# Retention feeding a four-expert attention layer: the queries and keys of two experts in the two halves of the rows

## The chip, the cores and the metric

The kernel runs on one core of a Trainium2 chip. Its metric is the device time of one launch in microseconds (us), by the median of several runs. A profile of one execution gives the engines' instructions: PE is TensorE's matmuls, PEld its loads of stationary tiles, DVE VectorE, ACT ScalarE, POOL GpSimd, and SP the engine that issues the DMAs.

## What is computed

A retention layer (a decaying running state per head) gives x. A mixture of four attention experts, of which two count for each token, gives the output. B = 4 batches, H = 8 heads, S = 768 tokens, D = 64; the model width is 512, and an expert's head width Hd is 64.

```python
def _attn_ref(q, k, v):
    gamma = 1.0 - 2.0 ** (-5.0 - np.arange(H, dtype=np.float32))
    for t in range(S):
        state = gamma[None, :, None, None] * state + np.einsum('bhd,bhe->bhde', k[:, :, t], v[:, :, t])
        y[:, :, t] = scale * np.einsum('bhd,bhde->bhe', q[:, :, t], state)
...
def _moe_ref(x, w_gate, wq, wk, wv, wo):
    logits = x @ w_gate
    ...
    for e in range(E):
        q = x @ wq[e]
        k = x @ wk[e]
        v = x @ wv[e]
        scores = scale * (q @ k.transpose(0, 2, 1))
        scores = np.where(causal, -1000000000.0, scores)
        scores = scores - scores.max(-1, keepdims=True)
        a = np.exp(scores)
        a /= a.sum(-1, keepdims=True) + 1e-09
        ye = a @ v @ wo[e]
        ...
            out += mask[..., None] * w[:, :, kk:kk + 1] * ye
```

## The kernel before

The tokens are worked in eight stages j of HS = 384 (NJ = 8; an odd stage is the second half of its batch), each of three chunks of 128. The experts go in two pairs p.

Precision comes from splitting: a factor is held as a rounded part (hi, type fp32r) and the rest (lo), and products are summed as hi*hi + hi*lo + lo*hi. Plain fp32 matmuls stay in the retention and in the attention's last product; a plain fp32 matmul is issued as two instructions.

The steps, with their lines:

- `h1`, `h2`, `kturn` (L405 to L549): the retention, in 64x64 tiles, four of them to the array.
- `proj` (L599): queries and keys of one expert together, 128 output rows, 12 matmuls of 384 columns. ACT rounds q (L605) and k (L607) out of the bank, DVE takes the rests (L610, L613), and copies on POOL and ACT (L625, L627) bring q and k into the other half of the rows, so that one 128-row matmul gives (k_hi + k_lo) times q_hi.
- `vgate` (L650): values and gate logits, 260 columns.
- `mpass` (L731, L744, L745): the score rows again with tokens of q on the partitions, one expert at a time, for each row's maximum, which DVE takes out of the bank (L734, L753). `mrow` (L781 to L787) turns the maxima into a row through DRAM; in the last stage matmuls (L774) do it.
- `score` (L857, L858): for each block of 128 keys and each expert, two matmuls; the second, of 65 rows, adds k_hi times q_lo and subtracts the maximum through a row of ones. ACT takes the exponential (L864): 384-wide blocks once per expert, narrower ones for both experts in one bank and one instruction.
- `av` (L905), `norm_a`, `norm_b`, `wout` (L1031): the product with v, the sums, the normalisation, the output.

`Recorder.op` collects these steps with their dependencies, and `schedule` emits them in the order of the table `ORDER`, found offline and written out by number. All engines' streams, the DMA queue of SP included, follow that one order; tiles of a pool go to whoever comes next in it. Seven PSUM banks (`ps`) serve all but the retention's state. Every PE step carries a `mode`: the shape into which the array is divided, such as 128x128 or 64x64 (rows x columns of one tile).

Of the kernel before, what the change touches and what calls it, by code (L numbers as in the profile page):

```python
# [252 lines left out]
def tile_retention_moe_attention(  # L253
# [330 lines left out]
    def proj(j, p, e):  # L584
# [724 lines left out]
```

## Time and profile before

| | us |
|---|---|
| median of 3 runs (lowest, highest) | 328.93 (328.56, 329.5) |
| profiled execution | 330.6 |
| its span | 328.7 |
| PE, PEld busy | 315.1, 279.2 |
| DVE, POOL, ACT busy | 200.7, 180.4, 162.2 |

The span is the part of the profiled execution between its first and its last instruction; 1.9 us lie around it. Shares of busy time are means over the whole span. A matmul's row shows its time through the array, so rows of following matmuls overlap; how long one holds the next up is the distance between their starts.

### The profile page before, as it was taken

The numbers are of one execution on the slowest core, as the hardware profiler recorded it, in microseconds if no ns is written. First come the engines' busy times: TensorE is split into PE (matmuls) and PEld (weight loads), VectorE is DVE, ScalarE is ACT, GpSimd is POOL, SyncE is SP. The second block draws the span as 40 slices with busy tenths as digits, with TensorE's granted clock in tenths as the row PEclk, the third lists the DMA queues.
The fourth block names the chain that finished last, engine by engine and source line by source line (L and its number), as shares of the span: only waits on it lengthen the run. The fifth ranks groups of instructions, "written<-read, shape, count | busy, mean of one in ns | idle before, by whom it ended". The sixth has DMA issues, their size and how long they took to land.

```text
span 328.7 us, 11866 instructions
## 1 busy us (share of the span) xinstructions
PE 315.1 (96%) x5060; PEld 279.2 (85%) x5060; DVE 200.7 (61%) x538; ACT 162.2 (49%) x376; POOL 180.4 (55%) x206
## 2 busy tenths in 40 slices
PE   4797999999999999999999999999999999999995
PEld 4487999998997899998997899988998899877673
DVE  2772588788744454595657255677564276688653
ACT  1410455463566255554553625564674417857532
POOL 2674344544398691946278964681397912816300
PEclk9997999999999999999999999999999999999999
DMA  6978272150723522553406322144300112013012
GB/s 222 353 251 256 68 255 69 71 181 23 237 75 131 163 74 95 210 122 95 130 10 223 133 76 81 54 162 152 84 1 4 50 38 71 15 61 79 35 64 96
DMA packets 15880, 37.54 MB, mean 114 GB/s; under 512 B 2034, under 2 KB 6214, under 8 KB 15828
## 3 DMA queue, kind: packets, MB, share of 16 engines
q1 hardware_dynamic: 15828, 36.79, 34.1%
q8 instruction: 39, 0.64, 0.7%
q14 instruction: 13, 0.11, 0.1%
HBM read 29.99 MB, written 6.79 MB: 112 GB/s over the span
## 4 chain that ended last, share of the span: by engine, by line
PE 92%; DMA 4%; DVE 1%; issue 1%; SPq 0%; ACT 0%; ACTq 0%
PE ps L599 21%; PE ps L905 11%; PE ps L650 11%; PE ps L1031 11%; PE ps L857 7%; PE ps L858 6%; PE ps_st L484 5%; PE ps L549 5%; DMA kv_t<-in_kv_dram 4%; PE ps L745 4%; PE ps L731 2%; PE ps L488 2%; PE ps L543 2%; PE ps L941 2%; PE ps L744 1%
## 5 line engine op out<-in xcount | busy, mean ns | idle before, releaser
L864 ACT ACTIVATE pt<-ps 128x384 f32<-128x384 f32 (+2 forms) x112 | 50.0, 491 | 19.2 <-PE ps L858 15.4
L753 DVE CUSTOM_DVE_ANT_0 scr<-ps,cmask 128x256 bf16<-128x256 f32 (+3 forms) x64 | 30.2, 486 | 35.9 <-PE ps L745 35.7
L599 PE MATMUL ps<-xh,qk_hi 128*128 128x384 f32 x128 | 44.6, 348 | 0.0
L599 PE MATMUL ps<-xl,qk_hi 128*128 128x384 f32 x128 | 43.5, 340 | 0.0
L599 PE MATMUL ps<-xh,qk_lo 128*128 128x384 f32 x128 | 43.5, 340 | 0.0
L857 PE MATMUL ps<-q,k 128*128 128x384 f32 (+2 forms) x144 | 43.5, 318 | 0.0
L858 PE MATMUL ps<-q,k 65*128 65x384 f32 (+2 forms) x144 | 42.5, 312 | 0.0
L905 PE MATMUL ps<-pt,vt 64*64 64x384 f32 (+2 forms) x576 | 41.7, 415 | 0.0
L886 POOL TENSOR_TENSOR ac<-ac,pt 128x256 f32<-128x256 f32 (+2 forms) x32 | 40.0, 1252 | 1.6
L438 POOL TENSOR_TENSOR qd<-qkT_t,tabs 128x512 f32<-128x512 f32 (+1 forms) x23 | 28.6, 1243 | 22.1 <-PE ps L488 18.1
L870 POOL TENSOR_SCALAR_AFFINE_SELECT pt<-pt 128x256 f32<-128x256 f32 x48 | 19.6, 418 | 27.3 <-ACT pt L864 23.2
L549 PE MATMUL ps<-qkT_t 64*64 64x64 f32 x768 | 28.1, 223 | 5.2 <-DMA qkT_t<-in_qkT_dram 4.9
L905 PEld LDWEIGHTS ps<-pt,vt 64*64 64x64 f32 x576 | 21.9, 133 | 12.1 <-issue 8.7
L549 PEld LDWEIGHTS ps<-qkT_t 64*64 64x64 f32 x768 | 26.0, 138 | 5.8 <-DMA qkT_t<-in_qkT_dram 4.9
L484 PE MATMUL ps_st<-kv_t 64*64 64x64 f32 x704 | 29.4, 221 | 0.6 <-DVE kv_t L423 0.3
L498 DVE TENSOR_TENSOR sblk<-ps_st,tabs 128x256 f32<-128x256 f32 x44 | 18.5, 421 | 18.6 <-PE ps_st L484 17.7
L484 PEld LDWEIGHTS ps_st<-kv_t 64*64 64x64 f32 x704 | 24.9, 134 | 5.7 <-issue 3.6
L650 PE MATMUL ps<-vg_hi,xl 128*128 128x260 f32 x96 | 27.6, 288 | 1.9 <-issue 1.9
L605 ACT ACTIVATE q<-ps 64x384 fp32r<-64x384 f32 x32 | 15.4, 480 | 28.0 <-PE ps L599 27.9
L488 PE MATMUL ps<-qd,sblk 64*64 64x64 f32 x704 | 29.2, 221 | 0.0
L857 PEld LDWEIGHTS ps<-q,k 128*128 128x128 f32 x144 | 27.4, 190 | 1.9 <-issue 0.9
L511 ACT ACTIVATE xh<-ps 128x512 fp32r<-128x512 f32 x24 | 14.3, 597 | 28.4 <-PE ps L488 28.2
(129 smaller groups left out, 838.0 us busy)
## 6 DMA issues: line engine op xcount, KB each, us to landing
qkT_t<-in_qkT_dram SPq DMA_DIRECT2D x24, 512.0 KB
kv_t<-in_kv_dram SPq DMA_DIRECT2D x23, 512.0 KB
out_dram<-ot SPq DMA_DIRECT2D x21, 256.0 KB
fe<-fd SPq DMA_DIRECT2D x28, 96.0 KB
pt<-in_wqk_dram SPq DMA_DIRECT2D x4, 256.0 KB
out_dram<-ot SPq DMA_DIRECT2D x6, 128.0 KB
...
```

What stands on the lines that cost most here:

```text
L484: nc.tensor.matmul(ST[b].t[rows(rt), s * D:(s + 1) * D], kvs(m, 0, s)[rows(rt)], kvs(m, 1, s)[rows(rt)], start=c == 0 and s == 0, stop=Fal ...
L488: nc.tensor.matmul(yo(m, rt, s), SB[m % 2][rows(rt), s], LD[g, 2].t[rows(rt), s, m % 2 * SC:(m % 2 + 1) * SC], start=m % 2 == 0 and s == 0 ...
L549: nc.tensor.matmul(ps.t[rows(rt), a:a + SC], qb.t[rows(rt), 1, s, t], qb.t[rows(rt), 0, s, t], start=True, stop=True)
L599: nc.tensor.matmul(pb.t[:, :HS], ww[:, kt, wsl], xx[:, kt], start=n == 0, stop=n == 11)
L650: nc.tensor.matmul(pb.t[:, :NV + E], xx[:, kt, sl], ww[:, kt], start=n == 0, stop=n == 11)
L753: lambda: nc.vector.tensor_tensor_reduce(scr.t[:, :n1], pb.t[:, :n1], K["cmask"][:, HS + C - n1:], 1.0, mx0.t[:, e, i:i + 1] if prior else ...
L857: nc.tensor.matmul(o, k1.t[:, e, ko:ko + C], q1.t[:, e, q0:], start=True, stop=False)
L858: nc.tensor.matmul(o, k2.t[:65, e, ko:ko + C], q2.t[:65, e, q0:], start=False, stop=True)
L864: lambda es=es, sb=sb, n=n: nc.scalar.activation(pt.t[:, es[0]:es[0] + n, q0:], sb.t[:, :n * w].rearrange("p (e t) -> p e t", e=n), AF.Exp ...
L886: op(eng, cost, lambda: en.tensor_tensor(ac.t[:, :, q0:], ac.t[:, :, q0:], pt.t[:, :, q0:], op=OP.add), r=[(pt, 0), (pt, 1), (ac, "b")], w ...
L905: nc.tensor.matmul(ob.t[e * 64:e * 64 + 64, q0:HS], VTB[kj].t[rr, ko // C, ee * 64:ee * 64 + 64], PTB[j, p, kb].t[rr, e, q0:], start=kb == ...
L1031: nc.tensor.matmul(wb.t, oo[:, sl], ww[:, p], start=n == 0 and p == 0, stop=n == 2 and p == NP - 1)
```

## The change

Queries of both experts of a pair are projected together, one expert into the upper 64 rows and the other into the lower; keys likewise (`_layouts` orders the weights so). Each projection is rounded by one ACT instruction over 128 rows and its rest is taken by one on DVE; the copies to the other half go. The pools Q1, Q2, K1, K2 of two experts' width become QH, QL, KH, KL of one. `mpass` and `score` issue matmuls of 64 rows in pairs, expert 0 from the upper rows into one bank and expert 1 from the lower rows into another; their shape is 64x128. `mpass` uses q_hi times k_hi alone. `score` has four steps: hi*hi, lo of q, lo of k, and a tile with one row of ones for each expert (`oner`) times the negated maxima (`mr`, two buffers, filled by two DMAs in place of one). The exponential is always one instruction per expert. In the last stage one set of three matmuls and one ACT copy brings both experts' maxima. The tiles for the exponentials (`pt`) grow from 8 to 12. `SUB` is empty, so its branches are never taken. The table of the order is new throughout.

```diff
-    Q1 = tag("q1", 3, [128, 2, HS], F32R)
...
+    QH = tag("qh", NQ, [128, HS], F32R)
+    QL = tag("ql", NQ, [128, HS], F32R)
+    KH = tag("kh", NK, [128, HS], F32R)
+    KL = tag("kl", NK, [128, HS], F32R)
+    MR = tag("mr", 2, [128, HS], F32R)
...
-    def proj(j, p, e):
+    def proj(j, p, t):
...
-        op("ACT", act_c(HS), lambda: nc.scalar.activation(q1.t[up, e], pb.t[up, :HS], AF.Copy), r=[(pb,)],
-           w=[(q1, "a", e)])
-        op("ACT", act_c(HS), lambda: nc.scalar.activation(k1.t[low, e], pb.t[low, :HS], AF.Copy), r=[(pb,)],
-           w=[(k1, "h", e)])
...
+        op("ACT", act_c(HS), lambda: nc.scalar.activation(th.t, pb.t[:, :HS], AF.Copy), r=[(pb,)], w=[(th,)])
+        op("DVE", dve_c(HS), lambda: nc.vector.tensor_tensor(tl.t, pb.t[:, :HS], th.t, op=OP.subtract),
+           r=[(pb,), (th,)], w=[(tl,)])
...
-    def mpass(j, p, e, i):
+    def mpass(j, p, i):
...
+        def mm(o, k, e, n):
+            nc.tensor.matmul(o, qh.t[rows(e), i * C:(i + 1) * C], k.t[rows(e), :n], start=True, stop=True)
...
+            for e in range(2):
+                mm(pb[e].t[:, n0:n1], kb, e, n)
+
+        op("PE", max(n * COL, 0.11) + n0 * COL + 0.01, fn, r=[(qh,), (kb,)] + ([(ka,)] if both else []),
+           w=[*[(x,) for x in pb], (mx, "n")], new=pb + ([mx] if new else []), mode="64x128", ni=8 if both else 4)
...
     def score(j, p, kb):
...
-                    nc.tensor.matmul(o, k1.t[:, e, ko:ko + C], q1.t[:, e, q0:], start=True, stop=False)
-                    nc.tensor.matmul(o, k2.t[:65, e, ko:ko + C], q2.t[:65, e, q0:], start=False, stop=True)
...
+            steps = [(kk[x].t, qq[y].t, ko) for x, y in ((0, 0), (0, 1), (1, 0))] + ([] if sub else [(oner, m.t, 0)])
+            for n, (k, q, o) in enumerate(steps):
+                for e in range(2):
+                    nc.tensor.matmul(sb[e].t[:, :w], k[rows(e), o:o + C], q[rows(e), q0:], start=n == 0,
+                                     stop=n == len(steps) - 1)
...
-        for es in ([(0, 1)] if w <= 256 else [(0,), (1,)]):
-            sb = Buf(PB)
-            n = len(es)
...
+            for e in range(2):
+                op("ACT", act_c(w),
+                   lambda e=e: nc.scalar.activation(pt.t[:, e, q0:], sb[e].t[:, :w], AF.Exp, scale=isc),
+                   r=[(sb[e],)], w=[(pt, e)])
...
     def mrow(j, p):
...
-            for e in range(2):
-                pb = Buf(PB)
...
-                    for i in range(CH):
-                        nc.tensor.matmul(pb.t[:65, i * C:(i + 1) * C], mz.t[:, e, i], nid, start=True, stop=True)
...
+                for i in range(CH):
+                    nc.tensor.matmul(pb.t[:65, i * C:(i + 1) * C], mz.t[:, i], nid, start=True, stop=True)
...
+            for e in range(2):
+                op("SP", 0.4,
+                   lambda e=e: nc.sync.dma_start(
+                       o.t[64 * e:64 * e + 1].bitcast(F32),
+                       md.t[e * CH:(e + 1) * CH].rearrange("c t -> (c t)")[None, :]),
+                   r=[(md,), ("mr0",)], w=[(o, e)], new=[] if e else [o], nbytes=1536)
...
 ORDER = """
-1 5 2 4 108 9 3 6 13 17 11 7 8 14 19 88 12 24 0 26 25 18 28 10 42 27 15 29 66 31 34 16 30 71 43 44 38 75 32 39 45 40
...
+6 1 22 2 5 3 4 9 13 12 19 14 7 17 8 11 88 18 24 87 0 26 25 20 10 42 27 36 15 28 75 29 43 66 31 38 16 32 30 40 39 37 44
...
```

What the new table does is seen in the built programs' streams. TensorE, maxima next to projections: before, two matmuls of `mpass` (L745, one expert each) stand between two projections (L599), all of 128x128.

```order
L599 MATMUL ps_141<-xh_73,qk_hi 128x384
L599 MATMUL ps_141<-xl_75,qk_hi 128x384
L599 MATMUL ps_141<-xh_73,qk_lo 128x384
L745 MATMUL ps_143<-k_0_82,q_0_76 128x384
L745 MATMUL ps_145<-k_0_82,q_0_76 128x384
L599 MATMUL ps_140<-xh_73,qk_hi 128x384
L599 MATMUL ps_140<-xl_75,qk_hi 128x384
L599 MATMUL ps_140<-xh_73,qk_lo 128x384
```

After, between two projections (L588) of a later stage (the last three and the first two rows of them), `mpass` (L685) issues two pairs; with qh and kh one row follows the other into two banks. One pair is over the stage's own keys (kh_87), the other over the half before (kh_85).

```order
L588 MATMUL ps_153<-xh_73,qk_hi 128x384
L588 MATMUL ps_153<-xl_75,qk_hi 128x384
L588 MATMUL ps_153<-xh_73,qk_lo 128x384
L685 MATMUL ps_152<-kh_87,qh_78 128x384
L685 MATMUL ps_151<-kh_87,qh_78 128x384
L685 MATMUL ps_150<-kh_85,qh_78 128x384
L685 MATMUL ps_149<-kh_85,qh_78 128x384
L588 MATMUL ps_148<-xh_72,qk_hi 128x384
L588 MATMUL ps_148<-xl_74,qk_hi 128x384
```

The maxima have moved out of a run of one shape into an island of their own: 128x128, 64x128, 128x128.

TensorE, scores: before, a stretch of `score` of the second stage, one bank for both experts at 256 columns, one for each at 384, then two maxima of a later stage; all of 128x128.

```order
L857 MATMUL ps_139<-q_1_77,k_1_83 128x256
L858 MATMUL ps_139<-q_1_80,k_1_88 128x256
L857 MATMUL ps_139<-q_1_77,k_1_83 128x256
L858 MATMUL ps_139<-q_1_80,k_1_88 128x256
L857 MATMUL ps_142<-q_1_77,k_1_83 128x384
L858 MATMUL ps_142<-q_1_80,k_1_88 128x384
L857 MATMUL ps_144<-q_1_77,k_1_83 128x384
L858 MATMUL ps_144<-q_1_80,k_1_88 128x384
L745 MATMUL ps_145<-k_2_84,q_2_78 128x384
L745 MATMUL ps_140<-k_2_84,q_2_78 128x384
```

After, one block of `score` (L832, 128 keys by 384 queries) with maxima (L685) ahead and behind: four steps, each once per expert, and all of 64x128.

```order
L685 MATMUL ps_148<-kh_85,qh_78 128x384
L685 MATMUL ps_149<-kh_85,qh_78 128x384
L832 MATMUL ps_151<-qh_79,kh_84 128x384
L832 MATMUL ps_152<-qh_79,kh_84 128x384
L832 MATMUL ps_151<-ql_83,kh_84 128x384
L832 MATMUL ps_152<-ql_83,kh_84 128x384
L832 MATMUL ps_151<-qh_79,kl_89 128x384
L832 MATMUL ps_152<-qh_79,kl_89 128x384
L832 MATMUL ps_151<-mr_94,oner 128x384
L832 MATMUL ps_152<-mr_94,oner 128x384
L685 MATMUL ps_147<-kh_87,qh_78 128x256
L685 MATMUL ps_150<-kh_87,qh_78 128x256
```

Two matmuls per expert and block have become four of half the rows, and maxima stand beside scores in the same shape.

SP, the first DMAs: before, the tables (L333) and two chunks of q and k (L382) lead, then half of the first k and v (L386) and the weights (L351).

```order
L333 DMA tabs<-in_tabs_dram 128x368
L382 DMA qkT_t_63<-in_qkT_dram 128x1024
L382 DMA qkT_t_64<-in_qkT_dram 128x1024
L386 DMA kv_t_66<-in_kv_dram 128x512
L351 DMA ac_117<-in_wvg_dram 128x260
L351 DMA pt_109<-in_wqk_dram 128x512
```

After, that half of the first k and v (L380) leads.

```order
L380 DMA kv_t_66<-in_kv_dram 128x512
L326 DMA tabs<-in_tabs_dram 128x368
L376 DMA qkT_t_63<-in_qkT_dram 128x1024
L376 DMA qkT_t_64<-in_qkT_dram 128x1024
L344 DMA ac_125<-in_wvg_dram 128x260
L344 DMA ot_135<-in_wvg_dram 128x260
```

It has moved ahead of the tables (L326) and of the first q and k (L376).

## Rows read from the trace of the kernel before

**Rows 1.** The page, engines (busy us, share, instructions), and the chain by engine.

```profile
PE 315.1 (96%) x5060; PEld 279.2 (85%) x5060; DVE 200.7 (61%) x538; ACT 162.2 (49%) x376; POOL 180.4 (55%) x206
...
PE 92%; DMA 4%; DVE 1%; issue 1%; SPq 0%; ACT 0%; ACTq 0%
```

**Rows 2.** Stretches: length, busy us (instructions) by engine, clock, DMA share, GB/s.

```profile
0.00:40.00 40.00, 30.43 (x691) 26.67 (x695) 18.97 (x37) 10.35 (x22) 20.48 (x30) 0.96 0.71 236
40.00:285.00 245.00, 245.00 (x4042) 223.61 (x4035) 152.59 (x418) 128.84 (x299) 147.82 (x161) 1.00 0.31 103
```

**Rows 3.** Waits of TensorE: sum in us, times, longest.

```profile
PE ps L549 <- DMA qkT_t<-in_qkT_dram: 4.9, 1, 4.9
PE ps L650 <- issue: 1.9, 1, 1.9
PE ps L1179 <- DVE xl L514: 1.8, 1, 1.8
```

**Rows 4.** Timeline of TensorE (start us, length): from 64x64 into 128x128.

```profile
59.48 0.22 PE L488 MATMUL ps<-qd,sblk 64*64 64x64 f32 x1
59.62 0.44 PE L857 MATMUL ps<-q,k 128*128 128x384 f32 x1
59.90 0.34 PE L858 MATMUL ps<-q,k 65*128 65x384 f32 x1
60.08 0.34 PE L731 MATMUL ps<-k,q 128*128 128x384 f32 x1
```

**Rows 5.** The same view: 256 columns, then from 128x128 into 64x64.

```profile
58.67 0.28 PE L857 MATMUL ps<-q,k 128*128 128x256 f32 x1
58.78 0.28 PE L858 MATMUL ps<-q,k 65*128 65x256 f32 x1
59.00 0.27 PE L484 MATMUL ps_st<-kv_t 64*64 64x64 f32 x1
```

**Rows 6.** The same view: 128 columns in a row.

```profile
101.80 0.28 PE L858 MATMUL ps<-q,k 65*128 65x128 f32 x1
101.91 0.28 PE L857 MATMUL ps<-q,k 128*128 128x128 f32 x1
```

**Rows 7.** Matmuls of the maxima: line, shape, count, busy us, mean ns.

```profile
L731 PE MATMUL ps<-k,q 128*128 128x384 f32 x32 | 10.8, 359 | 0.0
L745 PE MATMUL ps<-k,q 128*128 128x128 f32 (+2 forms) x96 | 24.3, 295 | 0.0
L744 PE MATMUL ps<-k,q 128*128 128x384 f32 x16 | 5.6, 367 | 0.0
```

**Rows 8.** Timeline of TensorE: groups of four 64x64 matmuls.

```profile
59.10 0.22 PE L484 MATMUL ps_st<-kv_t 64*64 64x64 f32 x1
59.11 0.22 PE L488 MATMUL ps<-qd,sblk 64*64 64x64 f32 x1
59.12 0.22 PE L484 MATMUL ps_st<-kv_t 64*64 64x64 f32 x1
...
59.16 0.22 PE L484 MATMUL ps_st<-kv_t 64*64 64x64 f32 x1
```

**Rows 9.** Timeline of the weight loads (PEld): the same groups.

```profile
59.16 0.14 PEld L484 LDWEIGHTS ps_st<-kv_t 64*64 64x64 f32 x1
...
59.22 0.14 PEld L484 LDWEIGHTS ps_st<-kv_t 64*64 64x64 f32 x1
```

**Rows 10.** Groups of ACT and DVE: exponential, evacuation of a projection.

```profile
L864 ACT ACTIVATE pt<-ps 128x384 f32<-128x384 f32 x80 | 35.5, 492 | 11.9 <-PE ps L858 10.4 <-DVE mx L753 0.5 <-POOL pt L870 0.3
L613 DVE TENSOR_TENSOR k<-ps,k 64x384 fp32r<-64x384 f32 x32 | 17.7, 559 | 6.5 <-ACT k L607 4.4 <-ACT q L605 1.4
L605 ACT ACTIVATE q<-ps 64x384 fp32r<-64x384 f32 x32 | 15.4, 480 | 28.0 <-PE ps L599 27.9
```

**Rows 11.** Stretches around the stop of TensorE at 26.5 us.

```profile
26.50:28.60 2.10, 0.22 (x3) 0.01 (x2) 0.00 (x0) 0.00 (x0) 0.11 (x1) 1.00 0.90 267
28.60:32.00 3.40, 3.40 (x12) 3.40 (x13) 0.00 (x0) 0.00 (x0) 1.94 (x2) 0.50 0.98 272
```

More of the change, by code (lines that the diff above doesn't have):

```diff
@@ L28 @@
 WARM = 8
-PACE = ()
-QP = True
-KP = False
+SUB = ()
+NQ = 4
 IDLE = (2, 4)
@@ L373, in tile_retention_moe_attention @@
     nid = sbuf.tile([128, 128], F32R, name="nid")
+    oner = sbuf.tile([128, 128], F32R, name="oner")
     K = {}
@@ L582, in stream_r @@
         return u
[L584 removed]
+    def proj(j, p, t):
         xh, xl = XT[j]
         hi, lo = W["qk"]
[L588 to L593 removed]
+        wsl = slice((p * 2 + t) * 128, (p * 2 + t + 1) * 128)
+        pb = Buf(PB)
+        th, tl = (KT if t else QT)[j, p] = (Buf(KH), Buf(KL)) if t else (Buf(QH), Buf(QL))
         def fn():
@@ L600, in fn @@
                     n += 1
-        op("PE", 12 * HS * COL, fn, r=xtok(xh) + xtok(xl) + wtok("qk"),
-           w=[(pb,), *[(t, "n") for t in (q1, q2, k1, k2)]], new=[pb, *new], mode="128x128", ni=24)
-        up, low = slice(0, 64), slice(64, 128)
-        op("ACT", act_c(HS), lambda: nc.scalar.activation(q1.t[up, e], pb.t[up, :HS], AF.Copy), r=[(pb,)],
-           w=[(q1, "a", e)])
-        op("ACT", act_c(HS), lambda: nc.scalar.activation(k1.t[low, e], pb.t[low, :HS], AF.Copy), r=[(pb,)],
-           w=[(k1, "h", e)])
-        op("DVE", dve_c(HS),
-           lambda: nc.vector.tensor_tensor(q2.t[up, e], pb.t[up, :HS], q1.t[up, e], op=OP.subtract),
-           r=[(pb,), (q1, "a", e)], w=[(q2, "x", e)])
-        op("DVE", dve_c(HS),
-           lambda: nc.vector.tensor_tensor(k1.t[up, e], pb.t[low, :HS], k1.t[low, e], op=OP.subtract),
-           r=[(pb,), (k1, "h", e)], w=[(k1, "q", e)])
-        each = j == NJ - 1
-        if not e and not each:
-            return
-        es = [e] if each else range(2)
-        a, b = es[0], es[-1] + 1
-        n = len(es) * HS
-        def turn(pool, d, s, r, w):
-            if pool:
-                op("POOL", pool_c(n), lambda: nc.gpsimd.tensor_copy(d(), s()), r=r, w=w)
-            else:
-                op("ACT", act_c(n), lambda: nc.scalar.activation(d(), s(), AF.Copy), r=r, w=w)
-        turn(QP and not each, lambda: q1.t[low, a:b], lambda: q1.t[up, a:b], [(q1, "a", y) for y in es],
-             [(q1, "b", y) for y in es])
-        turn(KP and not each, lambda: k2.t[up, a:b], lambda: k1.t[low, a:b], [(k1, "h", y) for y in es] + [("k2ones",)],
-             [(k2, "x", y) for y in es])
-    def qtok(j, p, e):
-        return [(QT[j, p][0], "a", e), (QT[j, p][0], "b", e)]
-    def ktok(j, p, e):
-        return [(KT[j, p][0], "q", e), (KT[j, p][0], "h", e)]
+        op("PE", 12 * HS * COL, fn, r=xtok(xh) + xtok(xl) + wtok("qk"), w=[(pb,), (th, "n"), (tl, "n")],
+           new=[pb, th, tl], mode="128x128", ni=24)
+        op("ACT", act_c(HS), lambda: nc.scalar.activation(th.t, pb.t[:, :HS], AF.Copy), r=[(pb,)], w=[(th,)])
+        op("DVE", dve_c(HS), lambda: nc.vector.tensor_tensor(tl.t, pb.t[:, :HS], th.t, op=OP.subtract),
+           r=[(pb,), (th,)], w=[(tl,)])
     def vgate(j, i):
@@ L722, in mpass @@
         mx, mx0 = MXB[j, p]
-        q1 = QT[j, p][0]
-        def lhs():
-            return q1.t[:, e, i * C:(i + 1) * C]
-        if half and i:
-            pa = Buf(PB)
-            ka = KT[j - 1, p][0]
-            op("PE", HS * COL, lambda: nc.tensor.matmul(pa.t[:, :HS], lhs(), ka.t[:, e], start=True, stop=True),
-               r=qtok(j, p, e) + ktok(j - 1, p, e), w=[(pa,), (mx0, "n")], new=[pa, mx0] if (e, i) == (0, 1) else [pa], mode="128x128", ni=2)
-            op("DVE", dve_c(HS),
-               lambda: nc.vector.tensor_reduce(mx0.t[:, e, i:i + 1], pa.t[:, :HS], axis=AX.X, op=OP.max),
-               r=[(pa,)], w=[(mx0, e, i)])
+        qh, kb = QT[j, p][0], KT[j, p][0]
@@ new lines, in mpass, with fa @@
+        ka = KT[j - 1, p][0] if half else None
+        def mm(o, k, e, n):
+            nc.tensor.matmul(o, qh.t[rows(e), i * C:(i + 1) * C], k.t[rows(e), :n], start=True, stop=True)
+        prior = half and i
+        if prior:
+            pa = [Buf(PB) for _ in range(2)]
+            def fa():
+                for e in range(2):
+                    mm(pa[e].t[:, :HS], ka, e, HS)
+            op("PE", HS * COL + 0.01, fa, r=[(qh,), (ka,)], w=[*[(x,) for x in pa], (mx0, "n")],
+               new=[*pa, mx0] if i == 1 else pa, mode="64x128", ni=4)
+            for e in range(2):
+                op("DVE", dve_c(HS),
+                   lambda e=e: nc.vector.tensor_reduce(mx0.t[:, e, i:i + 1], pa[e].t[:, :HS], axis=AX.X, op=OP.max),
+                   r=[(pa[e],)], w=[(mx0, e, i)])
@@ L736, in mpass @@
         n = (i + 1) * C
-        pb, scr = Buf(PB), Buf(SCR)
-        kb = KT[j, p][0]
         both = half and not i
         n0 = HS if both else 0
+        n1 = n0 + n
+        pb = [Buf(PB) for _ in range(2)]
         def fn():
             if both:
-                nc.tensor.matmul(pb.t[:, :HS], lhs(), KT[j - 1, p][0].t[:, e], start=True, stop=True)
-            nc.tensor.matmul(pb.t[:, n0:n0 + n], lhs(), kb.t[:, e, :n], start=True, stop=True)
-        n1 = n0 + n
-        op("PE", max(n * COL, 0.11) + n0 * COL, fn,
-           r=qtok(j, p, e) + ktok(j, p, e) + (ktok(j - 1, p, e) if both else []), w=[(pb,), (mx, "n"), (scr, "n")],
-           new=[pb, scr] + ([mx] if new else []), mode="128x128", ni=4 if both else 2)
@@ L751, in mpass @@
-        prior = half and i
-        op("DVE", dve_c(n1) + 0.05,
-           lambda: nc.vector.tensor_tensor_reduce(scr.t[:, :n1], pb.t[:, :n1], K["cmask"][:, HS + C - n1:], 1.0,
-                                                  mx0.t[:, e, i:i + 1] if prior else NEG, op0=OP.add, op1=OP.max,
-                                                  accum_out=mx.t[:, e * CH + i:e * CH + i + 1]),
-           r=[(pb,), ("cmask_t",)] + ([(mx0, e, i)] if prior else []), w=[(mx, e, i), (scr,)])
+                for e in range(2):
+                    mm(pb[e].t[:, :HS], ka, e, HS)
@@ new lines, in fn @@
+            for e in range(2):
+                mm(pb[e].t[:, n0:n1], kb, e, n)
+        op("PE", max(n * COL, 0.11) + n0 * COL + 0.01, fn, r=[(qh,), (kb,)] + ([(ka,)] if both else []),
+           w=[*[(x,) for x in pb], (mx, "n")], new=pb + ([mx] if new else []), mode="64x128", ni=8 if both else 4)
+        for e in range(2):
+            scr = Buf(SCR)
+            op("DVE", dve_c(n1) + 0.05,
+               lambda e=e, scr=scr: nc.vector.tensor_tensor_reduce(
+                   scr.t[:, :n1], pb[e].t[:, :n1], K["cmask"][:, HS + C - n1:], 1.0,
+                   mx0.t[:, e, i:i + 1] if prior else NEG, op0=OP.add, op1=OP.max,
+                   accum_out=mx.t[:, e * CH + i:e * CH + i + 1]),
+               r=[(pb[e],), ("cmask_t",)] + ([(mx0, e, i)] if prior else []), w=[(mx, e, i), (scr,)], new=[scr])
@@ L799, in stream_p @@
             for i in range(CH):
-                for e in range(2):
-                    mp[p].append((COST["m1"] if half else COST["m0"], lambda p=p, e=e, i=i: mpass(j, p, e, i)))
+                mp[p].append((COST["m1"] if half else COST["m0"], lambda p=p, i=i: mpass(j, p, i)))
             mp[p].append((COST["mrow"], lambda p=p: mrow(j, p)))
@@ new lines, in score, with fn @@
+        sub = j in SUB
+        sb = [Buf(PB) for _ in range(2)]
+        def fn():
+            steps = [(kk[x].t, qq[y].t, ko) for x, y in ((0, 0), (0, 1), (1, 0))] + ([] if sub else [(oner, m.t, 0)])
+            for n, (k, q, o) in enumerate(steps):
+                for e in range(2):
+                    nc.tensor.matmul(sb[e].t[:, :w], k[rows(e), o:o + C], q[rows(e), q0:], start=n == 0,
+                                     stop=n == len(steps) - 1)
+        op("PE", (3 if sub else 4) * max(w * COL, 0.11) + 0.01, fn,
+           r=[(x,) for x in (*kk, *qq)] + ([] if sub else [(m, 0), (m, 1) if j < NJ - 1 else (m, 0), ("oner",)]),
+           w=[*[(x,) for x in sb], (pt, "n")], new=[*sb, pt], mode="64x128", ni=4 * (3 if sub else 4))
@@ new lines, in score @@
+        if sub:
+            for e in range(2):
+                op("DVE", dve_c(w),
+                   lambda e=e: nc.vector.tensor_tensor(pt.t[:, e, q0:], sb[e].t[:, :w], m.t[:, e, q0:], op=OP.add),
+                   r=[(sb[e],), (m, e)], w=[(pt, e)])
+            op("ACT", act_c(2 * w),
+               lambda: nc.scalar.activation(pt.t[:, :, q0:], pt.t[:, :, q0:], AF.Exp, scale=isc),
+               r=[(pt, 0), (pt, 1)], w=[(pt, 0), (pt, 1)])
+        else:
+            for e in range(2):
+                op("ACT", act_c(w),
+                   lambda e=e: nc.scalar.activation(pt.t[:, e, q0:], sb[e].t[:, :w], AF.Exp, scale=isc),
+                   r=[(sb[e],)], w=[(pt, e)])
@@ L1216, in head, with mkone, mkmr @@
         wsplit(2)
-        for t in K2.tiles:
-            op("POOL", 0.73, lambda t=t: nc.gpsimd.memset(t[64:65].bitcast(F32), 1.0), w=[("k2ones",)])
+        def mkone():
+            nc.gpsimd.memset(oner.bitcast(F32), 0.0)
+            for e in range(2):
+                nc.gpsimd.memset(oner[64 * e:64 * e + 1].bitcast(F32), 1.0)
+        def mkmr():
+            for t in MR.tiles:
+                nc.gpsimd.memset(t.bitcast(F32), 0.0)
+        op("POOL", 0.6, mkone, w=[("oner",)])
+        op("POOL", 1.5, mkmr, w=[("mr0",)])
     head()
```

79 lines of the change are left out of this document (32 added, 47 removed), and 110 rows, old and new, of the table ORDER.

## The prediction

> **What bounds the kernel now.** I read the shares of the engines and the chain first, then the stretches, then the waits, and last the distances from one matmul's start to the next. TensorE is busy 96% of the span and carries 92% of the chain; the next engine, VectorE, has 61% [rows 1]. The stretches sharpen this: from 40 to 285 us TensorE is busy 245.00 of 245.00 us at a granted clock of 1.00, the 2.4 GHz level, while 40.00 less 30.43 = 9.6 us of its idle time lie in the first 40 us [rows 2], half of it the wait for the first load [rows 3]. So no wait is worth removing in the middle: only columns that TensorE no longer streams, or columns and pauses that it gains, move the end there. A busy row hides pauses, since a matmul's row outlasts the start of the next, so every price below is a distance between starts.
>
> **Prices of a matmul.** With 384 columns the next one starts 0.18 us later [rows 4]; with 256 columns 0.12 [rows 5]; with 128 columns 0.11 and not 0.06 [rows 6]. So a step costs its columns, or 0.11 us if that is more, which is the load of a 128-wide stationary tile.
>
> **Maxima (mpass): shorter.** Before, one expert at a time: 80 matmuls of 384 columns (L731 32, L744 16, a third of L745's 96), 32 of 256 and 32 of 128 (the other thirds) [rows 7]. 80 x 0.176 + 32 x 0.118 + 32 x 0.11 = 14.1 + 3.8 + 3.5 = 21.4 us, all on the path. After, the two experts sit in the two halves of the rows and write two banks. If both run at once, 10.7 us go. Are they at once? The 64x64 matmuls of the retention start four to a group, 0.01 us apart, and the next group follows 0.06 us after the first [rows 8], so the halves of the rows do work side by side there. Their loads do too: four fit into 0.06 us [rows 9], and a first load alone shows as 0.04 to 0.05 where nothing hides it (below). No row shows it for fp32r with 128 columns, hence rivals below.
>
> **Scores: even.** Before, each expert had two matmuls per key block (k_hi + k_lo times q_hi; k_hi times q_lo with the maximum as a 65th row). After, both experts have four (hi*hi, hi*lo, lo*hi, ones times maximum), each on 64 rows, two at a time: four steps per key block either way, 40 blocks of 384 columns, 16 of 256, 16 of 128. Twice as many matmuls are issued, but 0.01 us apart as above; I take 0.
>
> **The last stage's maxima:** 12 matmuls of 128 columns become 6: 6 x 0.11 = 0.7 us less.
>
> **Changes of shape: longer.** TensorE stops between shapes. Coming into 128x128 at 59.62, the first start is 0.14 us behind the last of a group that would have followed after 0.04, and the second comes 0.28 us on where later steps take 0.18 [rows 4]: 0.10 + 0.10 or 0.11, about 0.21 in all. Coming into 64x64 at 59.00, 0.22 instead of 0.12, and then 0.10 instead of 0.06 [rows 5, 8]: 0.14 to 0.15. The difference is the first load, which nothing hides: 128 columns or 64. In the order of before the shape changes 76 times (36 into 128x128, 29 into 64x64, 7 into 128x32, 4 into 128x64). In the new order it changes 124 times: 41, 34, 7, 4, and 38 into 64x128, since maxima and scores that stood inside a run of projections now break it. The new shape has 128 columns to load, so I price it like 128x128: (41 + 38 - 36) x 0.215 + 5 x 0.148 = 9.2 + 0.7 = 9.9 us more. From both sides: a change of rows alone (128x128 to 64x128 and back, 41 of the 124) has no row and might cost nothing, which takes 41 x 0.215 = 8.8 us off; or the two halves load one after the other, 38 x 0.11 = 4.2 us on.
>
> **ScalarE, VectorE, GpSimd: relief that earns nothing.** The evacuation of a projection drops from two ACT instructions of 64 rows (0.48 us each) and two on DVE (0.56) to one each of 128 rows: 32 x 0.48 = 15 us of ACT and 32 x 0.56 = 18 of DVE [rows 10], and the copies of L625 and L627 go as well. Against it, the exponentials of narrow blocks run once per expert. TensorE waited for none of these in the middle [rows 2], so I book 0.
>
> **Banks.** A score block or a maximum always takes two of the seven banks now, where narrow blocks took one. In a run of dense blocks ACT is the slower: a 384 block costs 2 x 0.49 = 0.98 us of ACT [rows 10] against 4 x 0.176 = 0.70 of TensorE, so ACT falls 0.28 us further behind with each, until no bank is free. Both orders have five runs of four to six blocks with only maxima between. Between 0 and 5 x 0.8 = 4 us; I take 0.5, near the low end, because in the same kind of runs before no idle row appears.
> The Trainium skill's page "TensorEngine Tiling (Array Packing)", section "Gotcha 1: PSUM Pressure", speaks against the change here: row tiles have to write to different banks and raise the demand on them. No run here shows it yet; by it the high end would stand, and the sum would be 3.5 us worse.
>
> **Start.** The first load of kv, half a chunk, now stands ahead of tables and qkT. The first matmul waits 4.9 us for qkT [rows 3]; 0.26 MB more at the 236 GB/s of the first stretch [rows 2] is 1.1 us. Against it, the first vgate stands ahead of the second chunk and fills a hole (1.8 us, for xl [rows 3]) with up to 12 x 0.12 = 1.4 us of work. I take 0. One idle matmul moved into the middle costs 0.2.
>
> **Sum.** -10.7 - 0.7 + 9.9 + 0.2 + 0.5 = -0.8 us. The profiled execution took 330.6 us, 328.7 of it span; 329.8 is 0.24% less, and on the median of 328.93 that gives 328.1 us.
>
> **Rivals.**
> *A. Rows alone change for little.* If 128x128 to 64x128 does not stop TensorE, up to 8.8 us come back: 319.5 to 325, around 322. For it: every change seen alters the columns, and part of its price is the load. Against it: every change seen stops TensorE for about 0.1 us ahead of the load, whatever the two shapes, hence a small chance.
> The skill's page "TensorEngine Tiling (Array Packing)", section "Key Properties", says that any change of tiling mode, not of a tile, drains the engine; the rows of columns agree, none shows rows alone. By it A fails and 328.1 stands.
> *B. Code arrives late (slower).* At 26.5 TensorE stopped for 2.1 us, put down to "issue" [rows 3], while DMA was at 0.90, and then ran 3.4 us at a granted clock of 0.50, 1.2 GHz [rows 11]: 2.1 + 1.7 = 3.8 us lost. I read it as the next piece of program behind the bulk loads. The change adds 286 matmuls and 286 loads to 10,120 instructions [rows 1], and the 64x64 matmuls, the densest in instructions, come sooner after one another early on. The place would be the first 50 us, where loads are still queued; one more stop of that kind adds 3.8 us: 332. It decides from a stop of some 2 us on, below which the sum absorbs it. If the old stop vanishes, the same price is a gain: 324.3.
> *C. The halves load in turn (slower).* Then a step takes two loads of 0.107 [rows 6], 0.214 us: 160 score steps of 384 at +0.038, 64 of 256 at +0.096, 64 of 128 at +0.104, and 40, 16, 16 of the maxima: 18.9 + 4.7 = 23.6 us more, 352. Against it: [rows 9].
> The skill's page "TensorE: Matmul & The Clock Gate", section "LDWEIGHTS (loading the stationary operand)", says that a load takes as long as its columns, whatever its rows. The 0.11 us of a 128-wide step agrees. It means that a 64x128 tile is no cheaper to load than a whole one, so that the step holds only while the two loads overlap.
> *D. The halves do not run at once in fp32r (the change does not do what it says).* The scores double: 160 x 0.176 + 64 x 0.118 + 64 x 0.11 = 42.8 us, and the 10.7 us are not gained: about 382. Against it: [rows 8].
>
> **How the numbers follow.** Forecast, 328.1, prices as above with small waits either way, 326.5 to 330: 0.55. A: 0.10. B, 330.5 to 333: 0.15. The banks' high end, 331.6: 0.06. The old stop gone: 0.05. C: 0.05. D: 0.04. A measurement of this kernel tells 0.3%, 1.0 us, from no change: below 327.9 is faster, above 329.9 slower. The forecast's own share I split 0.24 faster, 0.26 same, 0.05 slower. Faster: 0.24 + 0.10 + 0.05 = 0.39. Same: 0.26 + 0.01 of the banks' case = 0.27. Slower: 0.05 + 0.15 + 0.05 + 0.09 = 0.34. The range from 322 to 333 leaves out half of A, a little of B, and C and D, 0.16 together; the forecast's own is 326.5 to 330.
>
> **What would show it.** Right: starts of the score pairs 0.01 us apart with the next pair 0.18 us on at 384 columns; maxima at half their steps; a first start into 64x128 about 0.1 us late and a second again; TensorE still without an idle row from 40 to 285 us. Wrong: pairs 0.21 us apart (C) or 0.35 (D); a change from 128x128 to 64x128 without a pause (A); "issue" waits of a microsecond and slices of the clock below 9 (B); rows of TensorE that wait for the exponential (banks).

## The result

The changed kernel is slower. Before it took 328.75 us (median of 4 runs, 327.77 to 329.5), after it 332.89 us (median of 4, 331.5 to 333.98): a ratio of 1.0125, 95% interval 1.0077 to 1.0174, or 4.1 us. The forecast was 0.8 us of gain. The profiled execution of after took 334.0 us with a span of 332.3.

The page of after: engines (busy us, share of the span, instructions), the chain by engine, and the instruction queue with its packets.

```profile
PE 314.2 (95%) x5342; PEld 266.1 (80%) x5342; DVE 182.8 (55%) x506; ACT 131.6 (40%) x352; POOL 166.0 (50%) x192
...
q8 instruction: 42, 0.69, 0.9%
...
PE 89%; issue 4%; DMA 2%; POOL 2%; SPq 1%; ACT 1%; DVE 0%; POOLq 0%; ACTq 0%
```

Against [rows 1]: VectorE, ScalarE and GpSimd are relieved as forecast, and TensorE (PE) carries 89% of the chain instead of 92. What came in is "issue", 4% instead of 1: time in which an engine waited for nothing that the profile shows.

Stretches of after: length, then busy us (instructions) of PE, PEld, DVE, ACT, POOL, granted clock, DMA share, GB/s.

```profile
0.00:40.00 40.00, 29.14 (x732) 25.32 (x733) 18.34 (x36) 9.80 (x21) 16.43 (x28) 1.00 0.70 241
40.00:285.00 245.00, 241.87 (x4189) 209.79 (x4190) 133.10 (x380) 99.78 (x271) 136.52 (x146) 1.00 0.31 102
120.50:123.10 2.60, 0.41 (x9) 0.02 (x4) 0.57 (x1) 0.00 (x0) 2.60 (x3) 1.00 0.78 221
```

In [rows 2] the stretch from 40 to 285 us had 245.00 busy us of 245.00. Now 3.1 us are idle. The waits of TensorE in after (sum, times, longest) name them, where [rows 3] shows one wait of that kind, at 26.5 us:

```profile
PE ps L541 <- DMA qkT_t<-in_qkT_dram: 7.9, 1, 7.9
PE ps L888 <- issue: 2.2, 1, 2.2
PE ps L480 <- issue: 1.3, 1, 1.3
PE ps L607 <- issue: 0.8, 1, 0.8
PE ps L541 <- issue: 0.7, 1, 0.7
PE ps_st L476 <- issue: 0.5, 1, 0.5
```

The 2.2 us (ending at 123.08), the 0.8 us (at 85.14) and the last 0.17 us of the 1.3 (at 40.17) are the 3.1 us. The first load is waited for 7.9 us, where it was 4.9.

The pairs themselves do what they should. Timeline of TensorE in after (start us, length, line), into a score block of 64x128:

```profile
110.97 0.40 PE L888 MATMUL ps<-pt,vt 64*64 64x128 f32 x8
111.30 0.44 PE L832 MATMUL ps<-qh,kh 64*128 64x384 f32 x2
111.58 0.33 PE L832 MATMUL ps<-ql,kh 64*128 64x384 f32 x2
111.75 0.34 PE L832 MATMUL ps<-qh,kl 64*128 64x384 f32 x2
```

Two matmuls ("x2") start as one, the next pair 0.17 us on, as one 128-row matmul in [rows 4]; only the step behind the first pair is 0.28, the unhidden load.

### The profile page after: what moved, and what is told of

It is laid out like the page before. It is cut to its first block, busy times and chain, and to the rows that moved or that the text cites. A ratio compares the mean times of both kernels' runs of the same rounds, so it can differ in the third digit from the quotient of the medians.

```text
span 332.3 us, 12346 instructions
## 1 busy us (share of the span) xinstructions
PE 314.2 (95%) x5342; PEld 266.1 (80%) x5342; DVE 182.8 (55%) x506; ACT 131.6 (40%) x352; POOL 166.0 (50%) x192
## 4 chain that ended last, share of the span: by engine, by line
PE 89%; issue 4%; DMA 2%; POOL 2%; SPq 1%; ACT 1%; DVE 0%; POOLq 0%; ACTq 0%
PE ps L588 21%; PE ps L832 14%; PE ps L888 12%; PE ps L607 10%; PE ps L1014 10%; PE ps_st L476 5%; PE ps L541 5%; PE ps L685 5%; PE ps L480 2%; DMA pt<-in_wqk_dram 2%; PE ps L535 2%; PE ps L924 2%; PE ps L750 1%; PE ps L971 1%; POOL qk_lo L351 1%
## 5 line engine op out<-in xcount | busy, mean ns | idle before, releaser
L849 ACT ACTIVATE pt<-ps 128x384 f32<-128x384 f32 (+2 forms) x144 | 51.4, 421 | 15.7 <-PE ps L832 14.3
L588 PE MATMUL ps<-xh,qk_hi 128*128 128x384 f32 x128 | 45.1, 352 | 0.0
L588 PE MATMUL ps<-xh,qk_lo 128*128 128x384 f32 x128 | 43.1, 336 | 0.1
L588 PE MATMUL ps<-xl,qk_hi 128*128 128x384 f32 x128 | 43.0, 336 | 0.0
L719 DVE CUSTOM_DVE_ANT_0 scr<-ps,cmask 128x128 bf16<-128x128 f32 (+3 forms) x64 | 28.8, 486 | 16.7 <-PE ps L685 16.0
L888 PEld LDWEIGHTS ps<-pt,vt 64*64 64x64 f32 x576 | 20.4, 133 | 17.0 <-issue 14.0
L476 PE MATMUL ps_st<-kv_t 64*64 64x64 f32 x704 | 30.2, 222 | 0.6 <-issue 0.5
L951 POOL TENSOR_TENSOR on<-on,fe 128x384 f32<-128x384 f32 x14 | 15.1, 1088 | 26.8 <-DMA fe<-fd 26.8
L607 PE MATMUL ps<-vg_hi,xh 128*128 128x260 f32 x96 | 28.2, 293 | 0.0
L607 PE MATMUL ps<-vg_lo,xh 128*128 128x260 f32 x96 | 27.2, 283 | 0.4 <-POOL vg_lo L351 0.4
L535 PE MATMUL ps<-am,kv_t 64*64 64x64 f32 x768 | 27.6, 222 | 0.0
```

Of the source, the lines that this page charges most:

```text
L476: nc.tensor.matmul(ST[b].t[rows(rt), s * D:(s + 1) * D], kvs(m, 0, s)[rows(rt)], kvs(m, 1, s)[rows(rt)], start=c == 0 and s == 0, stop=Fal ...
L535: nc.tensor.matmul(yo(2 * g + u, rt, s), kvs(u + 2 * g, 1, s)[rows(rt)], amg.t[rows(rt), u, s], start=g % NC == 0 and u == 0 and s == 0, s ...
L588: nc.tensor.matmul(pb.t[:, :HS], ww[:, kt, wsl], xx[:, kt], start=n == 0, stop=n == 11)
L607: nc.tensor.matmul(pb.t[:, :NV + E], xx[:, kt, sl], ww[:, kt], start=n == 0, stop=n == 11)
L719: lambda e=e, scr=scr: nc.vector.tensor_tensor_reduce(scr.t[:, :n1], pb[e].t[:, :n1], K["cmask"][:, HS + C - n1:], 1.0, mx0.t[:, e, i:i + ...
L849: lambda e=e: nc.scalar.activation(pt.t[:, e, q0:], sb[e].t[:, :w], AF.Exp, scale=isc),
```

## The experiments

Comparisons below are between ratios to the kernel before; a thousandth is 0.33 us.

**The yardstick.** The changed kernel once more, without an edit.

> The changed kernel once more, as the yardstick for the three runs beside it. Both theories: 332.9 us, 1.0125 of the kernel before, within 1.008 to 1.017.

Measured: 1.0123 (1.0073 to 1.0173), 333.37 us. The loss repeats, and so do the five "issue" waits. Behind the one that ends at 121.90 (1.9 us) the clock fell in this profiled execution, which in after it did not (length, then busy us of PE, granted clock, DMA share, GB/s):

```profile
122.02:125.43 3.41, 3.41 (x27) 0.50 0.02 6
```

**The first loads put back.** Entry 6 of ORDER is the first half of kv, 5 the tables, 4 and 9 the first qkT loads.

```diff
-6 1 22 2 5 3 4 9 13
+1 22 2 5 3 4 9 6 13
```

> The changed kernel with one entry of its order moved: the load of kv's first half goes behind the tables and the first two qkT loads, as in the kernel before. Theory S (the 4 us are lost at the start and in stops where PE waits for nothing that the profile shows): the first matmul comes at 4.9 us again and not at 7.9; of these 3.0 us the trace of after had given back all but 1.1 by 20 us, so 331.8 us, 330 to 332.5. Theory P (the pairs cost more than they save, and the start is hidden): 332.9, within 0.5.

Measured: 1.0084 (1.0052 to 1.0117), 331.5 us: 1.3 us less than the yardstick, in the range of theory S but not clear of the noise, since the intervals overlap. Where the 3.0 us at the start are lost again is seen in the waits of this run, and then in two stretches, ahead of the second wait's end and behind it (columns as for the stretches of after). The profiled execution took 329.5 us, 2.0 less than the median, so it shows the places and not the balance:

```profile
PE ps L540 <- DMA qkT_t<-in_qkT_dram: 4.9, 1, 4.9
PE ps L540 <- issue: 2.1, 1, 2.1
```

```profile
19.00:21.80 2.80, 0.66 (x23) 0.52 (x19) 2.78 (x2) 0.00 (x0) 2.80 (x3) 1.00 0.84 280
22.35:25.76 3.41, 3.41 (x93) 3.29 (x86) 1.62 (x3) 0.19 (x1) 0.65 (x2) 0.50 0.45 181
```

The first matmul starts at 4.9 again; but the "issue" wait of 0.7 us has grown to 2.1 us, and behind it the granted clock is 0.50, the lower of its two levels (1.2 GHz), for 3.4 us. The 3.0 us themselves vary: in the seven profiles that keep the first loads of after, the first load is waited for 6.0 to 7.9 us.

**One projection moved.** 507 is one projection's 24 PE instructions, 458 the first of three attention groups.

```diff
-590 589 457 458
+590 589 457 507 458
...
-419 507 421
+419 421
```

> The changed kernel with one projection (24 PE instructions, 2.1 us, which stood at 124.7 us of the profiled execution) moved ahead of the three attention groups that start at 117.9 us; everything else stands as it was. PE's wait of 2.5 us at 120.5 us lies 2.7 us after the last 256 PE instructions began. Theory S: the moved projection lies where that wait was, since PE then has enough work in hand for as long as the wait takes; the wait goes, two more shape changes come (0.4 us): 330.8 us, 330.0 to 331.5. Theory P: the wait is of another kind or comes back elsewhere; with the two shape changes 333.3, within 0.5.

Measured: 1.0048 (1.0016 to 1.0081), 330.56 us: 2.5 us less than the yardstick, somewhat more than theory S expected. The moved projection is followed by the attention group that had waited 2.2 us (timeline of TensorE; the last column is the idle time before it and its cause):

```profile
118.82 0.34 PE L587 MATMUL ps<-xh,qk_lo 128*128 128x384 f32 x1
119.09 0.53 PE L887 MATMUL ps<-pt,vt 64*64 64x384 f32 x1
119.81 2.16 PE L887 MATMUL ps<-pt,vt 64*64 64x384 f32 x24 [0.19 <-issue]
```

**Both moves.**

```diff
-6 1 22 2 5 3 4 9 13
+1 22 2 5 3 4 9 6 13
...
-590 589 457 458
+590 589 457 507 458
...
-419 507 421
+419 421
```

> Both moves together. Theory S: the two gains add, 332.9 - 1.1 - 2.1 = 329.7 us, 328.5 to 331. Theory P: 333.3, within 0.5.

Measured: 1.0044 (1.0009 to 1.0079), 330.17 us: 2.6 us less than the yardstick, at the slow end of theory S and no more than the projection alone. The gains do not add, and the waits say why: TensorE reaches the next "issue" wait earlier and stands there longer, and from there to 26.0 us the granted clock is 0.50.

```profile
PE ps L540 <- DMA qkT_t<-in_qkT_dram: 5.2, 1, 5.2
PE ps L540 <- issue: 2.6, 1, 2.6
```

**Two loads later, PE's order untouched.** 737 and 738 are a qkT and a kv load that TensorE first needs after 160 us.

```diff
-465 470 737 455
+465 470 455
...
-458 738 592
+458 592
...
-543 655 514
+543 655 737 738 514
```

> The changed kernel with two loads moved in SP's order: those of qkT and kv that were issued at 117.2 and 119.6 us and are first used after 160 us go behind the next two projections; PE's order is left word for word. It asks what makes PE's wait of 2.5 us at 120.5 us so long. In the trace of after the transfer of 16 KB that brings PE's next instructions starts 3.0 us behind the 256th instruction there, with 0.7 MB of loads passing ahead of it; where no load is under way such a transfer starts after 0.4 to 1.2 us. Theory S: without these loads it starts about 2 us earlier, the wait falls to 0.3 to 0.7 us: 331.0 us, 330.3 to 332. If the wait has nothing to do with loads: 332.9, within 0.5.

Measured: 1.0054 (1.0021 to 1.0087), 331.18 us: 2.3 us less than the yardstick, and the wait at that attention group falls from 2.2 to 0.3 us with not one TensorE instruction moved:

```profile
118.52 1.47 PE L887 MATMUL ps<-pt,vt 64*64 64x384 f32 x13
120.26 1.19 PE L887 MATMUL ps<-pt,vt 64*64 64x384 f32 x12 [0.27 <-issue]
```

So the wait hangs on loads, though no data of theirs is used there. In after, two stretches of the DMA view (queue, packets, MB, share of 16 engines) show what is late:

```profile
DMA packets 195, 0.70 MB, mean 240 GB/s; under 512 B 25, under 2 KB 25, under 8 KB 195
...
q1 hardware_dynamic: 195, 0.70, 72.3%
...
DMA packets 148, 0.55 MB, mean 221 GB/s; under 512 B 16, under 2 KB 16, under 8 KB 147
...
q1 hardware_dynamic: 147, 0.54, 76.8%
q8 instruction: 1, 0.02, 2.3%
```

From 117.7 to 120.6 us (first three lines) only data moves; a packet of instructions starts behind 120.6 (the rest; a stretch of 120.60 to 120.70 has it already), and TensorE goes on at 123.08, 2.4 us later. In the run with the two loads moved the packet starts at 117.9, and TensorE goes on at 120.26, 2.3 us later. The page has 42 such packets for 2 x 5342 PE instructions, one for about 254. The stretch from 117.68 to 120.40 has 278 PE rows (those that reach over its ends count too), in 2.72 us:

```profile
117.68:120.40 2.72, 2.72 (x140) 2.19 (x138) 1.79 (x8) 1.22 (x4) 2.64 (x2) 1.00 0.74 242
```

TensorE ran through a whole piece of program before the next had come. Counting says the same: the five "issue" waits of after stand ahead of the matmul rows 351, 606, 733, 1750 and 2514 of its trace, about a multiple of 127 rows apart each time, which with their weight loads are 254 instructions. In the first new order of after (below), where the instructions come in another sequence, the three such waits of 1 us and more stand at rows 351, 3025 and 3662. The moved projection stretches the time that a piece lasts, the moved loads let the next one start earlier; each alone removes the wait but for 0.2 or 0.3 us.

**Maxima one after the other.** Both matmuls of a pair on the upper rows.

```diff
-            nc.tensor.matmul(o, qh.t[rows(e), i * C:(i + 1) * C], k.t[rows(e), :n], start=True, stop=True)
+            nc.tensor.matmul(o, qh.t[rows(0), i * C:(i + 1) * C], k.t[rows(0), :n], start=True, stop=True)
```

> The changed kernel with both matmuls of every maxima pair on the upper 64 rows (both then give the maxima of the first expert of the pair, which shifts the exponents of the second and leaves the work as it is): the two of a pair can no longer run at once; instructions, shapes and order stay. It prices the term of the maxima. Theory S, as the prediction had it: the halving of the maxima is worth 10.7 + 0.7 us, so 332.9 + 11.4 = 344.3, 342 to 346. If pairs of the maxima overlap only in part or other waits hide the gain: 333 to 340.

Measured: 1.0378 (1.0309 to 1.0448), 341.88 us: 8.4 us more than the yardstick (5.6 to 11.2 with the two intervals), a bit below the 342 to 346 expected. The edit touches `mpass` alone, so of the 11.4 us only the 10.7 apply. The run understates them, as its timeline shows where maxima (L685) stand between score blocks (L832):

```profile
92.89 0.27 PE L832 MATMUL ps<-mr,oner 64*128 64x128 f32 x2
93.00 0.38 PE L685 MATMUL ps<-kh,qh 64*128 64x384 f32 x1
93.00 0.43 PE L832 MATMUL ps<-qh,kh 64*128 64x384 f32 x1
93.23 0.34 PE L685 MATMUL ps<-kh,qh 64*128 64x384 f32 x1
```

The lower rows do not wait for the second maxima at 93.23: their score matmul, which comes later in the program, starts at 93.00, so part of the lost halving is hidden there.

**More shape changes, and their control.** wu is a tile of zeros; with rows(0) the added matmul changes the shape twice, on whole tiles it does not.

```diff
                     n += 1
+                    if n == 6:
+                        nc.tensor.matmul(pb.t[:, :64], wu[rows(0)], wu[rows(0), :64], start=False, stop=False)
```

> The changed kernel with a matmul of 64 rows, 128 columns of weights and 64 moving columns of zeros added to the middle of each of the 32 projections: 64 more shape changes between 128x128 and 64x128 and 32 small matmuls. It prices a change of the rows alone. Theory S, as the prediction had it: 0.215 us each, 64 x 0.215 = 13.8, and 32 times 0.03 to 0.11 for the matmul itself: 332.9 + 14.8 to 17.2 = 347.7 to 350.1. Rival A of the prediction (a change of the rows alone is free): 334 to 336.5. Theory P (changes cost more than their rows showed, 0.3 us): 353 to 356.

```diff
                     n += 1
+                    if n == 6:
+                        nc.tensor.matmul(pb.t[:, :64], wu, wu[:, :64], start=False, stop=False)
```

> The control to the run with more shape changes: the same 32 added matmuls of zeros, on all 128 rows, so that no shape changes. All theories: 32 times 0.03 to 0.11 us, 334 to 336.5 us; the difference to the other run is 64 shape changes.

Measured: 1.0481 (1.0412 to 1.055), 345.52 us, and 1.0262 (1.0195 to 1.0329), 338.11 us. Both missed: 2 to 5 us less than expected with changes, 1.6 more than the top without. The timelines (with changes, then the control) show the parts:

```profile
143.30 0.33 PE L588 MATMUL ps<-xh,qk_lo 128*128 128x384 f32 x1
143.57 0.20 PE L591 MATMUL ps<-wu 64*128 64x64 bf16 x1
143.70 0.44 PE L588 MATMUL ps<-xh,qk_hi 128*128 128x384 f32 x1
143.97 0.34 PE L588 MATMUL ps<-xl,qk_hi 128*128 128x384 f32 x1
```

```profile
136.05 0.34 PE L588 MATMUL ps<-xh,qk_lo 128*128 128x384 f32 x1
136.23 0.20 PE L591 MATMUL ps<-wu 128*128 128x64 bf16 x1
136.27 0.42 PE L588 MATMUL ps<-xh,qk_hi 128*128 128x384 f32 x1
136.53 0.34 PE L588 MATMUL ps<-xl,qk_hi 128*128 128x384 f32 x1
```

Into 64x128 the start comes after 0.27 instead of 0.18: 0.09. Back, after 0.13 instead of 0.04: 0.09. The step behind is 0.27 and 0.26: a load that nothing hides is 0.09 to 0.10 and stands in both, since a matmul of 64 columns hides no load either; that is what made the control dearer. Over all 32 places the two changes cost 0.20 us more than the control's matmul, 6.4 us of the 7.2 between the two runs. So a change of the rows alone stops TensorE for 0.09 us and leaves one load of 0.10 open: 0.19, close to the 0.215 that was used, and the run was mis-sized because its small matmul has no second step. Rival A falls.

**New orders for both kernels.** Only the table ORDER is new: a random search moved its entries and kept what the planner's own rules (`schedule`) found shorter, with 0.215 and 0.148 us for a change of shape, 4.2 us (up to 5.7 behind loads) for a piece of program, and with tables and the first two qkT loads held ahead of all other loads. It made two orders of each kernel. The changed kernel's come from a search 1.6 times as long, though the expectation on record for the kernel before has "from as long a search"; by the planner's rules the longer search came out within 0.02 us of the first order that was run for it, which no run shows. The first entries of the first order of the changed kernel, and of the first order of the kernel before:

```diff
-6 1 22 2 5 3 4 9 13 12
+5 1 4 2 9 0 3 7 8 23
```

> The changed kernel, its instructions as they are, with a new order on every queue: searched by the rules of its own planner, but with 0.215 us for a shape change into 128 columns and 0.148 into 64, as the traces show them, where the table in the kernel was made with 0.17 for both, with 4.2 us for PE's next 256 instructions and up to 1.5 more behind loads, and with tables and qkT first. 117 sets of one shape in place of 125. Theory S (order and start cost the changed kernel its 4 us; the pairs themselves gain a little): no wait of PE over 1 us after 40 us, first matmul at 4.9, some 325 us, 323 to 328. Theory P (the pairs lose by themselves): 329 to 333.

```diff
-1 5 2 4 108 9 3 6 13 17
+87 1 5 7 2 4 0 9 6 3
```

> The kernel before, its instructions as they are, with an order searched by the same rules and prices and from as long a search: 70 sets of one shape in place of 77. It tells the order from the pairs. Theory S: if pairs are worth the sum of the prediction (0.8 us), this run comes within 1 us of the changed kernel with its new order. Theory Q (the 47 more shape changes cost what the halved maxima save, and more): it comes 2 us or more below that run, at 321 to 325 us. If the order of before was already as good as such a search makes it: 328 to 329.

And the second ones:

```diff
-6 1 22 2 5 3 4 9 13 12
+5 1 0 86 7 2 23 4 24 3
```

> The changed kernel with a second order from the same search with another start: 118 sets of one shape. It tells whether the 0.989 of the first such order belongs to the kernel or to that one order. If to the kernel: 0.985 to 0.993 of the kernel before again, 324 to 327 us. If the order was a lucky one: 328 or more.

```diff
-1 5 2 4 108 9 3 6 13 17
+1 0 23 22 5 4 7 2 24 28
```

> The kernel before with a second order from the same search: 70 sets of one shape. If the pairs bring something when both kernels have an order of the same making, it stays 2 to 3 us above the changed kernel's: 0.995 to 1.001 of the kernel before, 327 to 329 us. If the first one was an unlucky order: 323 to 326 us, and the pairs bring nothing.

| kernel, order | median us | ratio to the kernel before | interval |
|---|---|---|---|
| after, as given | 332.89 | 1.0125 | 1.0077 to 1.0174 |
| after, new order | 325.45 | 0.9891 | 0.985 to 0.9932 |
| after, second new order | 326.03 | 0.9855 | 0.9816 to 0.9894 |
| before, new order | 328.21 | 0.9979 | 0.9952 to 1.0006 |
| before, second new order | 333.65 | 1.0097 | 1.0064 to 1.013 |

Each ratio is to the kernel before in the same round of runs: its median was 328.75 us beside after as given, 328.87 beside the first new orders and 330.44 beside the second.

The same instructions that lose 1.25% in the given order gain 1.1 and 1.45% in the new ones: both beat both kernels. For the kernel before, the search found nothing: S's "within 1 us" and Q both fail, and the third case, 328 to 329, holds; the changed kernel is the faster one here, by 2.9 us in the first orders. The second order of before lies outside both its cases. Nor did all of theory S for the changed kernel come true: its time did, but two "issue" waits of 1.1 and 1.0 us stand between 40 and 285 us in the first new order. The stretch from 40 to 285 us and then the waits of over 1 us in it, of the second new order of after (first two blocks) and of before (last two):

```profile
40.00:285.00 245.00, 243.59 (x4229) 210.95 (x4227) 138.14 (x396) 101.77 (x277) 138.69 (x149) 1.00 0.31 104
```

```profile
PE ps L587 <- issue: 1.2, 1, 1.2
```

```profile
40.00:285.00 245.00, 239.94 (x3922) 217.88 (x3921) 150.41 (x415) 120.90 (x287) 146.46 (x162) 1.00 0.30 100
```

```profile
PE ps L939 <- issue: 2.6, 1, 2.6
PE ps L486 <- POOL qd L436: 1.7, 1, 1.7
```

The kernel before can have such waits too; its 333.65 us carry 2.6 of "issue" and 1.7 of a wait for GpSimd. So these two orders of before do not bound what a good one would give.

All four new orders changed the start as well. The kernel has idle matmuls, on a tile of zeros (wu); eight of them now run while the first loads are on their way. TensorE in the first new order of after, and then two rows of after as given:

```profile
1.57 3.26 PE L1151 MATMUL ps<-wu 128*128 128x512 bf16 x8 [1.57 <-POOL wu L1101]
5.10 0.39 PE L540 MATMUL ps<-qkT_t 64*64 64x64 f32 x6 [0.27 <-DMA qkT_t<-in_qkT_dram]
...
12.46 0.32 PE L541 MATMUL ps<-qkT_t 64*64 64x64 f32 x2
12.57 0.32 PE L541 MATMUL ps<-qkT_t 64*64 64x64 f32 x2
```

As given, such groups start 0.11 us apart and last 0.32 us until the clock rises at 13.29 us, against 0.06 and 0.22 in [rows 8]: the lower level. In the new order the trace has the upper level from 4.36 us on, ahead of the first product with data. No run moved the idle matmuls alone.

A balance of the profiled executions, as an estimate from the starts of all of TensorE's rows (us; "work" is the time from start to start without idle time and idle matmuls, with stretches at the lower level counted half):

| kernel, order | span | work | idle matmuls | idle time | lost to the lower level | behind the last start |
|---|---|---|---|---|---|---|
| before, as given | 328.7 | 308.1 | 3.5 | 9.7 | 3.2 | 4.2 |
| after, as given | 332.3 | 308.0 | 3.4 | 14.1 | 2.7 | 4.1 |
| before, new order | 326.1 | 308.1 | 4.9 | 7.5 | 2.2 | 3.5 |
| after, new order | 324.0 | 307.1 | 4.5 | 8.8 | 0.0 | 3.7 |

So of the gain of the first new order of after, 8.3 us in these profiles, 5.3 are idle time and 2.7 the clock, and only 0.9 work (the idle matmuls took 1.1 more). Between the two first new orders the work differs by 1.0 us, and the clock by more, 2.2.

## Why the prediction was wrong

**Its sum of TensorE's work: nearly right.** Pairs start together and follow each other as one matmul did (C and D fall), a change of rows costs what a change of columns costs (A falls), and 124 changes stand in the trace. The halving of the maxima, 10.7 us in the sum, showed 8.4 in a run that understates it. By the balance above, work and idle matmuls together shrank by some 0.2 us, where maxima, last-stage maxima, shape changes and the idle matmul came to -1.3. One price is part of the difference: [rows 6] hold for matmuls of 128 columns one after the other, but among longer ones a maximum of 128 columns holds up the next matmul by 0.06 us and not 0.11, as here in before:

```profile
149.71 0.35 PE L744 MATMUL ps<-k,q 128*128 128x384 f32 x1
149.89 0.22 PE L745 MATMUL ps<-k,q 128*128 128x128 f32 x1
149.95 0.28 PE L781 MATMUL ps<-ident,mx 128*128 128x128 f32 x1
```

With 0.06 for the 32 of them, their halving is worth 0.8 us less. None of this makes the kernel slower.

**Banks: right, and smaller still.** No idle row of TensorE waits for the exponential in after, so none of the 0.5 us shows, and the high end of 4 us falls. The Trainium skill's page "TensorEngine Tiling (Array Packing)", section "Gotcha 1: PSUM Pressure", says that row tiling raises the pressure on the banks; it gives no price, and no wait here comes from it.

**Start: a wrong term.** Zero was booked: 1.1 us of later first matmul against 1.4 of a filled hole. The first matmul came 3.0 us later in the profile of after, and 1.1 to 3.0 in the seven with this start; putting the loads back gained 1.3 us, not clear of the noise. The step that failed was to price a load ahead of qkT by its bytes; what holds qkT up beyond them stays open.

**The middle: the step that decided.** "So no wait is worth removing in the middle" was true of before, and the sum carried it over to an order that had been made anew. There the 3.1 us of "issue" waits arose that the trace of before has nowhere between 40 and 285 us. Rival B had the mechanism, code that comes late behind loads, and its price (332) came within 1 us of the result, but it got 0.15, and its place was wrong: it looked to the first 50 us. That the price came so near is luck: it stood for 2.1 us of stop and 1.7 of half clock, and what came was a stop of 2.2 us without the half clock, a later start, and the loss of the old stop. The decisive wait is at 120.5 us, where a retention chunk of 256 instructions is followed by attention groups while two loads of 0.5 MB pass. Moving either end of this removes it, worth 2.3 to 2.5 us. The order of instructions was at hand and would have shown the place as one to look at: 256 PE instructions of short matmuls in a row, next to loads. The stop of before at 26.5 us did go, with its stretch at half clock (rival B's other side), but shorter ones at 23.5, 34.4 and 40.2 took its place.

**Where the 3.6 us are, and what stays open.** The spans of the two profiles differ by 3.6 us. TensorE's idle time in the first 40 us is +1.3 (10.9 against 9.6) and the middle +3.1. The half clock of 26.5 us is gone, -1.7, but the clock rises later behind the first matmul, after 5.4 us at the lower level instead of 3.2, which is +1.1. Work and idle matmuls are -0.2: together 3.6. With both moves the kernel is still 0.44% slower than before. It is not settled how much of the gain of the new orders is the pairs alone, and how much the start and the luck of an order.
